# Chunk 2 of a fused kernel: transposes on the matmul engine against a transposed load normalised in place

## The chip, the cores and the metric

The kernel runs on one core of one Trainium2 chip. The metric is the device time of one execution in microseconds, as a median of three runs. Five engines run their own queues of instructions in program order: TensorE (matmuls, PE in the profile; PEld is its loading of weights), VectorE (DVE), ScalarE (ACT), GpSimd (POOL) and SyncE (SP, which here only starts transfers). They wait for each other by semaphores.

## The reference, cut to what matters

```python
xn = layernorm(q)                                  # (1, 2048, 448), over the last axis
# branch A
k_shift = sum(k_pad[:, t:t + S] * shift_k[:, 3 - t] for t in range(4))
kv = k_shift * v
y  = irfft(rfft(kv, 2S) * rfft(ssm_k, 2S))[:S] + kv * ssm_D      # long causal convolution
A  = xn * y
# branch B
h   = xn @ w1 + b1                                 # 448 -> 1792
B   = (h * tanh(softplus(h))) @ w2                 # 1792 -> 448
return q + A + B
```

Everything is float32. There are S = 2048 positions and D = 448 columns.

## The kernel before, in words

**The dense branch.** The 2048 positions are cut into 8 chunks of 256 (`CH`), each chunk into two halves `jj` of 128. For each chunk the 1792 hidden columns are handled in 7 pairs of 128-column blocks. So there are 56 pairs; pair `i` is chunk `i // 7`, block pair `i % 7`. A float32 product is done as three products of rounded parts: weights are held as `w1h`, `w1l`, `w2h`, `w2l`, the normalised input as `XH` and `XL`, the activations as `ach` and `acl`. "High" is a rounded copy made by ScalarE, "low" is the rest, made by VectorE with a subtraction.

The program is a list of half steps, the slots `s`, written out by hand. Pair `i` has slots `2i` and `2i + 1`. In the even one TensorE does the first product, `g1_mm(i)` (L513). In the odd one ScalarE does the activation, `mish(i)` (L521) and the rounded copy (L85), VectorE the low part `acl` (L86), and TensorE the second product of the pair two steps back, `g2_mm(i - 2)` (L545 to L547), which sums over a chunk's 7 pairs in two accumulators `pg2`, one for each half. There are two such buffers in all, so a chunk's first `g2_mm` has to wait until the sum of the chunk before has been read. That is done by `g2_evac` (L552, VectorE): it adds the accumulators into the tile `Q[c]`, which holds the chunk of q. For chunk `c` it stands at the start of slot 14c + 18, one half step behind the last `g2_mm` of the chunk. `g2_out` then writes `Q[c]` out, and its buffer (there are three) goes to chunk `c + 3`.

**Two ways to the transposed input.** TensorE needs the normalised chunk with its columns on the partitions. Chunks below `NT` (3) go by the *transposes*: q is loaded (`ln_load`), VectorE takes mean and variance (L407, L410, L413), GpSimd raises to the power -0.5 (L416) and normalises (L420, L424), then `ln_T` transposes each half by four matmuls against an identity (L465) into an accumulator bank, from which ScalarE copies `XH` (L477) and VectorE subtracts `XL` (L475). Chunks from `NT` on go by a *transposed load*: `xT_load` reads q already transposed on the host (512 KB, L435), `nt_stats` takes the same moments, `nt_store` writes mean and factor to a scratch in memory (2 KB, `MR`, L443), `nt_row` reads them back as a row broadcast to all partitions (L446, 128 KB, one for each half) into `idr`, `nt_norm` subtracts and multiplies by the row (two VectorE operations of 128x512 a half, L452), and `nt_split` makes `XH` (L459) and `XL` (L460). The rows lie in the same tile as the identity, behind the constants `f1`.

The slots of these steps come from `NT_AT`, `NT_SOON` or an entry of `NT_HOW`: counted from `b`, the start of the chunk before (one slot behind it for chunks below 5), `q` is the slot of `ln_load`, `x` of `xT_load`, `stats` of the moments, `flush` of the slot by which they are all in the queue, and `row`, `norm` and `split` have one slot for each half. Moments are put into a list, `drip`; a call `dv()` behind most VectorE operations takes one of them out.

**The convolution branch** shares the first half of the time. `h` (the filter) and `kv` are brought to the frequency domain in 8 groups each: `f1_mm` (L147, TensorE, into the banks `pq` and `pr`), `f1_fold` (L153 ScalarE, then two VectorE operations, L157), `f1_out` (a transfer to `Dh` or `Dkv`). A kv group first needs the four taps and the product with v: VectorE operations L190 to L203, the last of them L203; one multiplication of each group is handed to GpSimd (`taps_pool`, L183). The groups' slots are `H_AT` and `KV_AT`; kv group 7 has slot 59. From slot 66 on come the frequency products (`hv_mm`, `prod`, `i1_mm`), and at the end the way back (`i2_mm`, `gate`).

Within a slot the queues get: `plan` of that slot, the products and activations, then `plan2` of that slot ("after"). Engines run far apart: VectorE is often a few us behind, SP as far ahead as buffers allow.

Of the kernel before, what the change touches and what calls it, by code (L numbers as in the profile page):

```python
# [17 lines left out]
NP = NF // 2  # L18
# [11 lines left out]
I2_AT = {100: ((6, 7, 0, 1), 92, (95, 97, 98, 99), (0, 2, 0, 1)),  # L30
         108: ((2, 3, 4, 5), 101, (104, 105, 106, 107), (0, 1, 0, 1))}
LATE = 2
NT = 3
NT_AT = {"q": -5, "x": -1, "stats": -2, "flush": 0, "row": (4, 8), "norm": (7, 10), "split": (8, 11)}
NT_SOON = dict(NT_AT, row=(4, 5), norm=(4, 7), split=(6, 8))
NT_HOW = {c: NT_SOON for c in (4, 7)}
NT_HOW[3] = dict(NT_SOON, q=-9, stats=-3, flush=-2)
NT_HOW[5] = dict(NT_AT, q=-8, stats=-4, flush=-2)
WARM_N = (448, 448, 448)
FILL_N = (224, 112, 96)  # L40

# [2 lines left out]
def tile_kernel(ctx: ExitStack, tc, q, qT, k, v, sk, hT, sD, w10, w1, w2, c_fib, c_g, c_gi, c_i2, out):  # L44
# [20 lines left out]
    E = dp.tile([NJ * 4, 64, D], F32, name="E")  # L65
    MR = {c: dp.tile([2, CH], F32, name="MR") for c in range(NT, NCHUNK)}

# [8 lines left out]
    def rs(c):  # L76
        return rstd[:, 2 * c:2 * c + 2] if c < NT else mv[:, 2 * c:2 * c + 2, 1]

# [26 lines left out]
    def dv(n=1):  # L105
        for _ in range(n):
            if drip:
                drip.pop(0)()
# [193 lines left out]
    def late(c):  # L302
        return c >= NCHUNK - LATE
# [84 lines left out]
    def ln_load(c, eng=None):  # L388
        Q[c] = mp.tile([128, 2, D], F32, name="qt", tag="qt", bufs=3)
        if c:  # L390
            nc.sync.dma_start(Q[c], q[:, 2 * c:2 * c + 2])
        else:
            for jj in range(2):
                nc.sync.dma_start(Q[c][:, jj], q[:, jj])

    def xn_tile():
        return mp.tile([128, 4, CH], F32, name="xn", bufs=1)

    def ln_parts(c):
        st = mp.tile([128, 2, 6], F32, name="bst", bufs=2)  # L400
        ve = mp.tile([128, 2], F32, name="ve", bufs=2)
        if c < NT:
            XN[c] = xn = xn_tile().rearrange("p a b -> p (a b)").rearrange("p (j d) -> p j d", j=2)
# [24 lines left out]
    def ln_stats(c):  # L428
        stats, aggr, eps, power, norm, tail, ve = ln_parts(c)
        drip.extend([lambda: stats(0), lambda: stats(1), lambda: aggr(0), lambda: aggr(1), lambda: eps(0, 2),  # L430
                     lambda: [f(*a) for f, *a in ((power, 0, 2), (norm, 0), (tail, 0, 1), (norm, 1), (tail, 1, 2))]])
# [47 lines left out]
    def ln_T(c, jj):  # L479
        if jj == 0:  # L480
            dv(len(drip))
            x_tiles(c)
        p = pg()
        transposes(c, jj, p)
        for lo in range(2):
            x_split(c, jj, p, lo)
# [4 lines left out]
    pairs = [(c, p) for c in range(NCHUNK) for p in range(NP)]  # L491

    def g1_mm(i):
        c, p = pairs[i]
        XH, XL = XS[c]
        pt = [(bank(GB[i]) if i in GB else pg()).rearrange("p (a b) -> p a b", a=2) for _ in range(2 if i == 0 else 1)]
        ps = [pt[n % len(pt)][:, n] for n in range(2)]
        mm = [[], []]
        for n in range(2):
            f = 2 * p + n  # L500
            fs = slice(128 * f, 128 * f + 128)
            hh, hl, lh = ([(w[:, kt, fs], x[:, kt]) for kt in range(3)] for w, x in ((w1h, XH), (w1h, XL), (w1l, XH)))
            th, tl = ((w1h[:, 3, fs], x[:, 3]) for x in (XH, XL))
            mm[n] = [(n, *m) for m in hh + lh + [th] + hl + [tl]]

            if 0 < i < NP:
                mm[n] = [(n, *m) for m in hh + hl + lh + [th, tl]]
        if i == 0:
            seq = mm[0][:7] + mm[1][:3] + mm[0][7:] + mm[1][7:10] + mm[1][3:7] + mm[1][10:]
        else:  # L510
            seq = mm[0] + mm[1]
        for n_, (n, l, r) in enumerate(seq):
            nc.tensor.matmul(ps[n], l, r, start=all(m[0] != n for m in seq[:n_]), stop=all(m[0] != n for m in seq[n_ + 1:]))  # L513
        P1[i] = ps

    def mish(i):
        p = pairs[i][1]
        ps = P1.pop(i)
        a = mp.tile([128, 2, CH], F32, name="a", bufs=2)
        for n in range(2):  # L520
            nc.scalar.activation(a[:, n], ps[n], AF.Mish, bias=b1t[:, 2 * p + n:2 * p + n + 1])  # L521
            if i == n == 0:
                w1_hi(2)
        if i == 0:
            w1_lo(2)
        ah = mp.tile([128, 2, CH], F32R, name="ach", bufs=3)
        al = mp.tile([128, 2, CH], F32R, name="acl", bufs=3)
        AHL[i] = ah, al
        if 2 * i + 1 in hv:
            held.append(lambda: split(ah, al, a))  # L530
        else:
            split(ah, al, a)
            dv()

    def g2_mm(i, jjs=(0, 1)):
        c, p = pairs[i]
        ah, al = AHL[i]
        for n in range(2):
            f = 2 * p + n
            for jj in jjs:  # L540
                if f == 0:
                    P2[c, jj] = g2p.tile([128, 512], F32, name="pg2")
                ps = P2[c, jj][:, :D]
                cs = slice(128 * jj, 128 * jj + 128)
                nc.tensor.matmul(ps, ah[:, n, cs], w2h[:, f], start=f == 0, stop=False)  # L545
                nc.tensor.matmul(ps, ah[:, n, cs], w2l[:, f], start=False, stop=False)  # L546
                nc.tensor.matmul(ps, al[:, n, cs], w2h[:, f], start=False, stop=f == NF - 1)  # L547

    def g2_evac(c, jjs=(0, 1)):
        x = Q[c]  # L550
        for jj in jjs:
            V.tensor_add(x[:, jj], P2.pop((c, jj))[:, :D], x[:, jj])  # L552
            dv()
            if late(c):
                nc.sync.dma_start(out[:, 2 * c + jj], x[:, jj])
# [4 lines left out]
    def mlp_slot(s):  # L560
        i, half = divmod(s, 2)
        n = len(pairs)
        j = i - G2_LAG
        if half == 0:
            if i < n:
                c, p = pairs[i]
                if c + 1 < NT:
                    if p == 0:
                        ln_load(c + 1)
                    if p == (3 if c in (0, 2) else 2):  # L570
                        ln_stats(c + 1)
                    if c == 0:
                        dv(len(drip))
                    if p == NP - 1:
                        ln_T(c + 1, 1)
                g1_mm(i)
        else:
            if i < n:
                c, p = pairs[i]
                if p == NP - 2 and c + 1 < NT:  # L580
                    ln_T(c + 1, 0)
                if s not in hv:
                    mish(i)
            if 0 <= j < n - 1:
                g2_mm(j)
            elif j == n - 1:
                for jj in range(2):
                    g2_mm(j, (jj,))
                    g2_evac(pairs[j][0], (jj,))
# [43 lines left out]
    for o in range(NO):  # L633
        s, d = OCT_AT[0] + OCT_AT[1] * o, OCT_AT[1]
# [33 lines left out]

    for c in range(NT, NCHUNK):
        at_ = NT_HOW.get(c, NT_AT)  # L670
        b = 2 * NP * (c - 1) + (1 if c < 5 else 0)
# [19 lines left out]
    warm = g2p.tile([128, 512], F32, name="pg2")  # L691
    for n in WARM_N:
        nc.tensor.matmul(warm[0:8, 0:n], wz, wz[:, 0:1].to_broadcast([128, n]), start=True, stop=True)
# [49 lines left out]
    plan.setdefault(5, []).insert(0, (f1_out, (Dh, H_HEAD, "h", nc.gpsimd)))  # L743
    for s in range(nslots):
        j = s // 2 - G2_LAG - 1
        if s % 2 == 0 and j >= 0 and pairs[j][1] == NP - 1:
            g2_evac(pairs[j][0])
        if s in hv:
            mish(s // 2)
        for fn, args in plan.pop(s, ()):  # L750
            fn(*args)
        mlp_slot(s)
        fns = plan2.pop(s, ())
        for fn, args in fns:
            if fn is i1_out:
                fn(*args)
        for fn, args in fns:
            if fn is not i1_out:
                fn(*args)
# [69 lines left out]
```

## Time and profile before

| | |
|---|---|
| median of 3 runs | 359.3 us (358.9 to 359.31) |
| the profiled execution | 359.25 us, of which the span from first to last instruction is 357.4 |
| mean granted TensorE clock | 0.998 |
| TensorE busy | 351.4 us, 98% |
| VectorE busy | 270.6 us, 76% |
| ScalarE busy | 156.8 us, 44% |
| GpSimd busy | 73.1 us, 20% |
| moved by DMA | 83.27 MB, 233 GB/s |

The span is also cut in 40 equal slices of 8.9 us, with a digit for the busy tenths of each. A group of instructions has its line, engine, operation, the tiles written and read, the shape, a count, and behind the bar the busy us and the mean ns of one; behind the second bar stands the engine's idle time just before them, and what ended it. In a timeline a row has its start, its length and the same names; two instructions of one kind in succession share a row (x2). Matmuls overlap, so the cost of one is read from the distance between starts, not from its length.

### The profile page before, as it was taken

What the parts mean: (1) busy time and instruction counts of PE and PEld (TensorE: products, weight loads), DVE (VectorE), ACT (ScalarE), POOL (GpSimd) and SP (SyncE); (2) the same over time, 40 slices, a digit from 0 to 9 for tenths busy, and PEclk for the clock granted to TensorE, in tenths of its full rate; (3) what the DMA queues carried; (4) which work ended last, traced back from release to release, by engine and by line L of the source; (5) the groups of instructions that cost most, each with busy time, mean ns of one, the idle gap of its engine ahead of it and who ended that gap; (6) DMA issues with size and microseconds to landing.
All of it is one profiled execution on the core that took longest, in us unless ns stands there. A gap on an engine that the chain in (4) does not pass through costs nothing.

```text
span 357.4 us, 7437 instructions
## 1 busy us (share of the span) xinstructions
PE 351.4 (98%) x3092; PEld 289.6 (81%) x3092; DVE 270.6 (76%) x375; ACT 156.8 (44%) x267; POOL 73.1 (20%) x78
## 2 busy tenths in 40 slices
PE   8999999999999999999999999999999999999995
PEld 2988888888888988888987757766775699979794
DVE  5989748999999999999537756756963933788941
ACT  3976652344243242342333453445445443354470
POOL 2037002942220240212000031011031116040030
PEclk9999999999999999999999999999999999999999
DMA  7998976949659537664869669999895387989086
GB/s 245 340 388 294 408 297 167 348 120 265 201 166 314 164 108 168 222 160 105 243 203 342 220 169 296 242 275 311 282 265 122 84 237 275 405 312 281 19 117 140
DMA packets 30691, 83.27 MB, mean 233 GB/s; under 512 B 3137, under 2 KB 15810, under 8 KB 30658
## 3 DMA queue, kind: packets, MB, share of 16 engines
q1 hardware_dynamic: 21842, 47.82, 39.7%
q0 software_dynamic: 4928, 22.95, 22.7%
q10 hardware_dynamic: 3888, 12.03, 12.8%
q8 instruction: 24, 0.39, 0.4%
q14 instruction: 9, 0.07, 0.1%
HBM read 54.34 MB, written 28.45 MB: 232 GB/s over the span
## 4 chain that ended last, share of the span: by engine, by line
PE 94%; DMA 2%; DVE 1%; ACT 1%; SPq 0%; issue 0%
PE pg L513 22%; PE pg L545 13%; PE pg L547 12%; PE pg L546 12%; PE pq L513 7%; PE pp L513 5%; PE pr L513 4%; PE pq L147 4%; PE pr L236 3%; PE pp L236 3%; PE pp L275 2%; DMA kr<-in_w_dram 2%; PE pq L236 2%; PE pr L275 1%; PE pp L329 1%; DVE st L157 1%
## 5 line engine op out<-in xcount | busy, mean ns | idle before, releaser
L545 PE MATMUL pg<-w2h,ach 128*128 128x448 f32 x224 | 82.6, 369 | 0.6 <-DVE qt L552 0.6
L547 PE MATMUL pg<-w2h,acl 128*128 128x448 f32 x224 | 81.4, 363 | 0.0
L546 PE MATMUL pg<-w2l,ach 128*128 128x448 f32 x224 | 81.2, 362 | 0.0
L86 DVE TENSOR_TENSOR acl<-a,ach 128x512 fp32r<-128x512 f32 x56 | 38.5, 688 | 32.1 <-ACT ach L85 31.8
L521 ACT ACTIVATE a<-pg,b1t 128x256 f32<-128x256 f32 x66 | 27.9, 473 | 66.6 <-PE pg L513 46.7
L513 PE MATMUL pg<-XH,w1h 128*128 128x256 f32 x264 | 52.8, 283 | 0.1
L545 PEld LDWEIGHTS pg<-w2h,ach 128*128 128x128 f32 x224 | 41.9, 187 | 12.2 <-issue 7.9
L513 PEld LDWEIGHTS pg<-XH,w1h 128*128 128x128 f32 x264 | 41.4, 188 | 7.2 <-issue 5.6
L547 PEld LDWEIGHTS pg<-w2h,acl 128*128 128x128 f32 x224 | 42.1, 188 | 2.4
L546 PEld LDWEIGHTS pg<-w2l,ach 128*128 128x128 f32 x224 | 42.1, 188 | 2.4
L513 PE MATMUL pg<-XL,w1h 128*128 128x256 f32 x264 | 42.9, 277 | 0.0
L157 DVE TENSOR_TENSOR st<-pq,st 128x896 f32<-128x896 f32 x32 | 34.8, 1087 | 4.5 <-ACT st L153 3.9
L513 PEld LDWEIGHTS pg<-XL,w1h 128*128 128x128 f32 x264 | 35.9, 188 | 0.0
L85 ACT CAST ach<-a 128x512 fp32r<-128x512 f32 x56 | 34.8, 621 | 1.7
L513 PE MATMUL pg<-XH,w1l 128*128 128x256 f32 x198 | 33.5, 278 | 0.0
L183 POOL TENSOR_TENSOR x<-kr,skb 128x896 f32<-128x896 f32 x8 | 17.0, 2129 | 68.2 <-PE pr L147 26.2
L513 PEld LDWEIGHTS pg<-XH,w1l 128*128 128x128 f32 x198 | 27.6, 188 | 0.0
L200 DVE TENSOR_TENSOR x<-x 128x896 f32<-128x896 f32 x24 | 26.2, 1090 | 1.6 <-POOL x L183 0.8
L521 ACT ACTIVATE a<-pq,b1t 128x256 f32<-128x256 f32 x20 | 8.4, 472 | 31.8 <-PE pq L513 31.8
L286 POOL DMA_DIRECT2D E<-qe x14 | 8.7, 629 | 63.1 <-ACT qe L283 63.1
L153 ACT COPY st<-pr 128x896 f32<-128x896 f32 x16 | 14.5, 907 | 14.1 <-PE pr L147 8.2
L416 POOL TENSOR_TENSOR mv<-ve,mhalf 128x2 f32<-128x2 f32 x5 | 5.0, 1008 | 72.0 <-DVE ve L413 72.0
(138 smaller groups left out, 608.5 us busy)
## 6 DMA issues: line engine op xcount, KB each, us to landing
Dkv<-st ACTq DMA_DIRECT2D x16, 448.0 KB, 5.3
ah<-Dh SPq DMA_DIRECT2D x8, 896.0 KB, 7.7
av<-Dkv SPq DMA_DIRECT2D x8, 896.0 KB, 8.5
e<-E POOLq DMA_DIRECT2D x8, 896.0 KB, 7.3
E<-qe POOLq DMA_DIRECT2D x14, 448.0 KB, 6.3
kr<-in_k_dram SPq DMA_DIRECT2D x10, 448.0 KB, 6.2
Dh<-st ACTq DMA_DIRECT2D x10, 448.0 KB, 6.6
x<-in_hT_dram SPq DMA_DIRECT2D x8, 448.0 KB, 6.1
```

The costliest lines, as they stand in the source:

```text
L85: nc.scalar.copy(h, raw)
L86: V.tensor_sub(l, raw, h)
L153: nc.scalar.copy(st[:, 1], o)
L157: f(st[:, n], e, st[:, 1])
L183: nc.gpsimd.tensor_mul(o, KR[g - u // 2], skb[:, u:u + 1].to_broadcast([128, 2, D]))
L200: V.tensor_add(KV[g], KV[g], o)
L236: nc.tensor.matmul(p[32 * t:32 * t + 32, r, :D], g[rs, t, c], a[rs, t], start=True, stop=True, tile_position=(64 * r, 32 * t))
L513: nc.tensor.matmul(ps[n], l, r, start=all(m[0] != n for m in seq[:n_]), stop=all(m[0] != n for m in seq[n_ + 1:]))
L521: nc.scalar.activation(a[:, n], ps[n], AF.Mish, bias=b1t[:, 2 * p + n:2 * p + n + 1])
L545: nc.tensor.matmul(ps, ah[:, n, cs], w2h[:, f], start=f == 0, stop=False)
L546: nc.tensor.matmul(ps, ah[:, n, cs], w2l[:, f], start=False, stop=False)
L547: nc.tensor.matmul(ps, al[:, n, cs], w2h[:, f], start=False, stop=f == NF - 1)
```

## The change

Chunk 2 goes by the transposed load instead of the transposes (`NT` is 2). Its steps are those of `NT_SOON`, with the splits in other slots. As `b` is 15 for chunk 2, this gives: `ln_load` slot 10 (before, 14), the moments in slots 13 to 15 (before, from 18), `xT_load` slot 14, the rows in slots 19 and 20, the normalisation behind slots 19 and 22, the splits behind slots 23 and 25. Before, the transposes stood in slots 25 and 26. Chunk 2's first product is in slot 28, as before.

And `g2_evac` of chunk 2 (`EVAC_SOON`) is moved from the start of slot 46 to the end of the products of slot 45, behind the last `g2_mm` of the chunk; so it stands ahead of what follows slot 45.

```diff
-NT = 3
+NT = 2
 NT_AT = {"q": -5, "x": -1, "stats": -2, "flush": 0, "row": (4, 8), "norm": (7, 10), "split": (8, 11)}
 NT_SOON = dict(NT_AT, row=(4, 5), norm=(4, 7), split=(6, 8))
 NT_HOW = {c: NT_SOON for c in (4, 7)}
+NT_HOW[2] = dict(NT_SOON, split=(8, 10))
 NT_HOW[3] = dict(NT_SOON, q=-9, stats=-3, flush=-2)
 NT_HOW[5] = dict(NT_AT, q=-8, stats=-4, flush=-2)
+EVAC_SOON = 2,
...
             if 0 <= j < n - 1:
                 g2_mm(j)
+                if pairs[j][1] == NP - 1 and pairs[j][0] in EVAC_SOON:
+                    g2_evac(pairs[j][0])
...
-        if s % 2 == 0 and j >= 0 and pairs[j][1] == NP - 1:
+        if s % 2 == 0 and j >= 0 and pairs[j][1] == NP - 1 and pairs[j][0] not in EVAC_SOON:
             g2_evac(pairs[j][0])
```

## The prediction

> **What bounds the kernel now.** I read the page first, then busy time by stretch, then the waits and the timeline where engines meet.
>
> ```profile
> span 357.4 us, 7437 instructions
> ...
> PE 351.4 (98%) x3092; PEld 289.6 (81%) x3092; DVE 270.6 (76%) x375; ACT 156.8 (44%) x267; POOL 73.1 (20%) x78
> ...
> DVE  5989748999999999999537756756963933788941
> ...
> PE 94%; DMA 2%; DVE 1%; ACT 1%; SPq 0%; issue 0%
> ```
>
> By the page TensorE is the bound: 98% busy, 94% of the chain. But VectorE's digits are nines from the 8th slice to the 19th (8.9 us each), so its 76% is a mean of two regimes. The same by stretch (columns: PE, PEld, DVE, ACT, POOL busy us, clock, DMA share, GB/s):
>
> ```profile
> 40.00:53.60 13.60, 13.60 (x103) 12.22 (x103) 7.01 (x8) 6.91 (x12) 0.00 (x0) 1.00 0.84 339
> 53.60:61.40 7.80, 7.80 (x64) 6.61 (x63) 6.64 (x14) 2.40 (x5) 0.93 (x1) 1.00 0.69 176
> 61.40:168.60 107.20, 106.65 (x813) 95.10 (x811) 104.72 (x148) 38.84 (x72) 32.02 (x19) 1.00 0.65 193
> 168.60:353.00 184.40, 184.40 (x1832) 146.00 (x1832) 117.82 (x152) 81.47 (x136) 27.50 (x40) 1.00 0.80 234
> ```
>
> From 61.40 to 168.60 both engines are full: TensorE idles 0.55 us, VectorE 2.48 us in 107.20. Before it VectorE is half idle (7.01 of 13.60), behind it TensorE never stops. Which of the two sets the pace in the full stretch is seen where TensorE waits for VectorE:
>
> ```profile
> PEld pq L147 <- DVE x L203: 0.2, 1, 0.2
> ```
> ```profile
> 167.51 1.09 DVE L203 TENSOR_TENSOR x<-x 128x896 f32<-128x896 f32 x1
> ```
> ```profile
> 168.66 0.59 PE L147 MATMUL pq<-x,con 32*64 32x448 f32 x2
> ```
> ```profile
> 135.84 1.14 DVE L552 TENSOR_TENSOR qt<-pg,qt 128x448 f32<-128x448 f32 x2
> ```
> ```profile
> 136.60 0.44 PE L545 MATMUL pg<-w2h,ach 128*128 128x448 f32 x1 [0.55 <-DVE qt L552]
> ```
>
> The last kv product (group 7, L203) ends at 168.60; its first-stage matmuls start at 168.66 and are listed as having waited for it. So at 168.6 TensorE has no slack against VectorE. At 136.60 it even stands 0.55 us, waiting for chunk 2's sum with q to free the accumulator of chunk 3. VectorE's queue runs without a real break from the fold at 61.40 to the product at 168.60, and it is VectorE's sum of work there that decides.
>
> **The change, part by part.** *TensorE loses chunk 2's eight transposes.*
>
> ```profile
> 73.88 0.60 PE L465 MATMUL pg<-con,xn 128*128 128x128 f32 x4
> 74.23 0.45 PE L545 MATMUL pg<-w2h,ach 128*128 128x448 f32 x1
> 74.52 0.37 PE L546 MATMUL pg<-w2l,ach 128*128 128x448 f32 x1
> 74.72 0.36 PE L547 MATMUL pg<-w2h,acl 128*128 128x448 f32 x1
> ...
> 77.76 0.66 PE L465 MATMUL pg<-con,xn 128*128 128x128 f32 x4
> 78.17 0.60 PE L513 MATMUL pg<-XH,w1h 128*128 128x256 f32 x3
> ```
>
> Start to start the two groups hold 0.35 (73.88 to 74.23) and 0.41 us (77.76 to 78.17); the first product behind the first takes 0.29 instead of the 0.20 of its neighbour. About 0.85 us, all on TensorE.
>
> *VectorE gets four normalising operations (L452), and its statistics move forward.*
>
> ```profile
> 47.60 0.69 DVE L86 TENSOR_TENSOR acl<-a,ach 128x512 fp32r<-128x512 f32 x1 [2.59 <-ACT ach L85]
> ...
> 61.40 1.09 DVE L157 TENSOR_TENSOR st<-pq,st 128x896 f32<-128x896 f32 x1 [1.09 <-ACT st L153]
> ...
> 64.63 0.69 DVE L86 TENSOR_TENSOR acl<-a,ach 128x512 fp32r<-128x512 f32 x1
> 65.24 0.98 DVE L193 TENSOR_TENSOR x<-kr,skb 128x448 f32<-128x448 f32 x1
> ...
> 70.52 0.97 DVE L193 TENSOR_TENSOR x<-kr,skb 128x448 f32<-128x448 f32 x1
> ...
> 77.68 0.62 DVE L193 TENSOR_TENSOR x<-kr,skb 128x448 f32<-128x448 f32 x1
> ...
> 103.88 1.41 DVE L452 TENSOR_TENSOR xn<-xn,con 128x512 f32<-128x512 f32 x2
> 105.22 1.08 DVE L157 TENSOR_TENSOR st<-pq,st 128x896 f32<-128x896 f32 x1
> ```
> ```profile
> 63.98 0.62 ACT L85 CAST ach<-a 128x512 fp32r<-128x512 f32 x1
> ```
> ```profile
> 63.53 3.37 POOL L420 TENSOR_SCALAR xn<-qt,mv,rstd 128x448 f32<-128x448 f32 x1
> ...
> 67.96 4.21 POOL L420 TENSOR_SCALAR xn<-qt,mv,rstd 128x448 f32<-128x448 f32 x1
> ```
> ```profile
> L460 DVE TENSOR_TENSOR XL<-xn,XH 128x512 fp32r<-128x512 f32 x10 | 6.9, 687 | 3.2 <-ACT XH L459 3.1
> ...
> L407 DVE BATCH_NORM_STATS2 bst<-qt 128x6 f32<-128x448 f32 x16 | 9.6, 618 | 2.8 <-DMA qt<-in_q_dram 2.7
> ```
> ```profile
> 81.00 0.68 DVE L475 TENSOR_TENSOR XL<-pg,XH 128x512 fp32r<-128x512 f32 x1
> ```
> ```profile
> 83.26 0.52 PE L513 MATMUL pg<-XH,w1h 128*128 128x256 f32 x3
> ```
>
> A pair of L452 holds VectorE 1.34 us (103.88 to 105.22). The statistics, now in slots 18 to 20, go to slots 13 to 15, into the 2.59 us idle before 47.60: free. The first pair stands after slot 19, just ahead of the fold at 61.40, where VectorE idles 1.09 us for ScalarE's copy; the two leaving statistics add 0.62 each, so 1.34 fits: free, with 1.09 + 1.24 − 1.34 = 1.0 us left. The second pair stands after slot 22, behind the product at 68.92 (a row below) and so inside the full stretch: +1.34. The two XL subtractions stay at the same price (0.69 against 0.68 us); they only read SBUF instead of an accumulator, as does ScalarE's cast ahead of each, and ScalarE has time (38.84 of 107.20).
>
> A wait could arise where chunk 2's first products need its low halves. The last XL now starts at 81.00; in the new order it stands behind the same products and comes 0.6 us later, done by 82.3. TensorE starts the chunk at 83.26 now, 0.85 sooner then, so at 82.4, and takes seven products of the high halves first, some 0.8 us at the spacing of this row's three (0.52 for three with the last one's run-out). Covered, by 0.8 us or so.
>
> What comes back: twice in this stretch L193 takes 0.98 and 0.97 us where its like takes 0.62, each time while GpSimd normalises chunk 2 (63.53 to 66.90, 67.96 to 72.17). Those two operations go away, and with them 0.36 + 0.35 = 0.71 us. A short operation ahead of 64.63 leaves too, but there VectorE waits for ScalarE's cast (63.98 + 0.62 = 64.60), so that gives nothing. Net for VectorE at 168.6: 1.34 − 0.71 = **+0.63 us**. Bounds: −0.1, if GpSimd cost other rows as much again; +1.34, if the two long rows have another cause.
>
> [...]
>
> *The sum with q of chunk 2* (L552 at 135.84) goes ahead of one 896-column product in VectorE's queue (of the size of L190's, 1.08 us, in a row below), and the write of its result and the reload of its buffer move with it. With VectorE late by 0.63 it still starts some 0.4 us sooner than now, which shortens the wait at 136.60. But TensorE then only arrives earlier at 168.66, where it waits for L203: worth nothing at the end. The same holds for the 0.85 us of transposes.
>
> *Queues.*
>
> ```profile
> L416 POOL TENSOR_TENSOR mv<-ve,mhalf 128x2 f32<-128x2 f32 x5 | 5.0, 1008 | 72.0 <-DVE ve L413 72.0
> ```
> ```profile
> DMA to landing us min/median/max: 3.8/5.2/10.0
> ```
> ```profile
> DMA to landing us min/median/max: 3.4/3.8/9.3
> ```
> ```profile
> 61.55 0.42 SPq L173 DMA_DIRECT2D kr<-in_k_dram  x1
> ```
> ```profile
> 68.92 1.08 DVE L190 TENSOR_TENSOR x<-kr,skb 128x896 f32<-128x896 f32 x1
> ```
> ```profile
> kr<-in_k_dram SPq DMA_DIRECT2D x10, 448.0 KB, 6.2
> ```
>
> GpSimd loses two normalisations and two copies of 64 columns and keeps the power. New transfers: the 512 KB of transposed q, the 2 KB of moments (L443, landing times 3.4/3.8/9.3) and two rows (L446, 3.8/5.2/10.0). GpSimd is empty from 40 to 53.6, so the moments leave by about 48.5 (47.6 at the latest for VectorE, 1.0 for the power), land at 52.3 and the row at 57.5, by medians. It is wanted at 59.1 (61.40 less the pair's 1.34 and the 1.0 left over); lateness up to 60.1 is free. The transposed q is asked for in slot 14, once chunk 1's last transposes have released its buffer, five slots ahead of use; the loads of h, k and v queued behind it on SP wait for that too, and are used three to nine slots later. Chunk 2's own q is asked for four slots sooner and passes the loads of slots 11 and 12 on SP, which land one place later, in a stretch in which VectorE is half idle. The second row waits on SP's queue for the first pair (60.4 by the above), ahead of the loads of q, h, k and v that follow there; I take 0.4 us later for them, one more issue of the length of the one shown. k at 61.55 lands at 67.8 by its median, then 68.2; VectorE wants it at 68.92 − 0.36 = 68.6. Hidden, by 0.4.
>
> **Sum.** The profiled execution took 359.25 us (span 357.4), the median is 359.3. The terms: transposes −0.85 and the wait at 136.6 up to −0.55, both used up by waiting at the last kv product; that product +1.34 − 0.71. TensorE starts group 7's matmuls 0.6 us later than at 168.66 and from there has no idle time to give (184.40 of 184.40): 359.25 + 0.6 = **359.8**.
>
> **Rivals.** (1) *Faster: TensorE keeps what it is relieved of.* That needs VectorE's last kv product to come at least 1.4 us sooner than I have it. Price: 0.85 + 0.55, so 357.8. For it: 98% and 94% of the page. Against: the wait at 168.66. [...] (2) *GpSimd's normalisation cost VectorE nothing:* the full 1.34, so 360.6. For it: most rows beside L420 have their usual length. (3) *Slower by a late row:* in a stretch with the DMA engines 0.84 busy the moments take their worst 9.3 us: 48.5 + 9.3 + 5.2 = 63.0 for the first row. It decides once the row lands behind 60.1; at 63.0 the fold that now starts at 61.40 starts at 64.3, 2.9 us late, of which nothing is made up before 168.6: 359.8 + 2.9 = 362.7.
>
> **How the numbers follow.** Forecast 0.55 (own range 359.3 to 360.4), rival 1 0.16, rival 2 0.18, rival 3 0.11. A measurement tells about 0.2% (0.7 us) from no change: 358.6 and 360.0 are the limits. The forecast lies close to the upper one and gives 0.38 within, 0.16 slower, 0.01 faster; rivals 2 and 3 are slower but for 0.01, rival 1 faster. So faster 0.17, same 0.39, slower 0.44. The range 358.4 to 361.2 takes in forecast, rival 2, half-kept gains and a slightly late row.
>
> **What would show it.** Right: no transposes between 73 and 79; L193 at 0.62 in both places; the last L203 ends near 169.2, with TensorE's wait before it of 1 us or so; the wait at 136.6 shorter or gone; VectorE idle under 2.5 us in its full stretch. Wrong: L203 ends before 168.6 (rival 1), or both L193 stay long (2), or the first L452 waits for con<-MR past 60.1 (3). A k load after 68.6 would add its lateness to all.

## The result, and the profile after

The changed kernel is slower: a median of 362.9 us (362.54 to 363.82, 4 runs) against 359.1 (358.9 to 359.31, 4 runs), a ratio of 1.0106 with the interval 1.0094 to 1.0119. The forecast was 359.8, the range 358.4 to 361.2. The profiled execution took 363.07 us, with a span of 361.1. The loss is not the clock's alone: three of the four executions after have a mean granted clock of 0.994 to 0.995, the fourth has 1.000 and took 362.54. In the kernel after, line numbers are two higher than in the kernel before.

VectorE's timeline after, from just behind chunk 2's moments to the last kv product (start, length, line, operation, and in brackets the idle time and what ended it):

```profile
47.31 0.69 DVE L88 TENSOR_TENSOR acl<-a,ach 128x512 fp32r<-128x512 f32 x1 [1.39 <-ACT ach L87]
...
60.12 1.42 DVE L454 TENSOR_TENSOR xn<-xn,con 128x512 f32<-128x512 f32 x2 [1.14 <-DMA con<-MR]
61.47 1.08 DVE L159 TENSOR_TENSOR st<-pq,st 128x896 f32<-128x896 f32 x1
...
65.48 0.62 DVE L195 TENSOR_TENSOR x<-kr,skb 128x448 f32<-128x448 f32 x1
...
71.21 1.09 DVE L192 TENSOR_TENSOR x<-kr,skb 128x896 f32<-128x896 f32 x1 [2.31 <-DMA kr<-in_k_dram]
72.22 1.41 DVE L454 TENSOR_TENSOR xn<-xn,con 128x512 f32<-128x512 f32 x2
...
74.15 0.62 DVE L195 TENSOR_TENSOR x<-kr,skb 128x448 f32<-128x448 f32 x1
...
171.28 1.09 DVE L205 TENSOR_TENSOR x<-x 128x896 f32<-128x896 f32 x1
```

Set against the same operations before, each start gives the lag so far, and each difference a term:

| operation | before | after | lag | what was added since the row above |
|---|---|---|---|---|
| low part `acl` | 47.60 | 47.31 | −0.29 | a different start of this execution |
| fold | 61.40 | 61.47 | +0.07 | 0.36: the first pair waits for its row |
| first long L193 | 65.24 | 65.48 | +0.24 | 0.17: mostly a gap of 0.20 behind GpSimd's multiplication |
| product L190 | 68.92 | 71.21 | +2.29 | 2.41 for k, −0.36 because L193 (now L195) takes 0.62, not 0.98 |
| second long L193 | 70.52 | 74.15 | +3.63 | 1.34: the second pair |
| last kv product | 167.51 | 171.28 | +3.77 | −0.35 for L193, +0.49 (below) |

The two executions differ by 363.07 − 359.25 = 3.82. So the loss is complete at the last kv product, and the largest part is one wait of VectorE for k. Why k was late is seen in the timelines of GpSimd, which sends the moments, and of SP, which starts the loads in its order:

```profile
47.04 0.77 POOL L445 DMA_DIRECT2D MR<-mv  x1 [0.29 <-POOL mv L418]
```
```profile
55.49 0.33 SPq L448 DMA_DIRECT2D con<-MR  x1
...
61.57 0.32 SPq L448 DMA_DIRECT2D con<-MR  x1
61.98 1.51 SPq L393 DMA_DIRECT2D qt<-in_q_dram  x1
63.59 0.37 SPq L135 DMA_DIRECT2D x<-in_hT_dram  x1
64.02 0.42 SPq L175 DMA_DIRECT2D kr<-in_k_dram  x1
```
```profile
DMA to landing us min/median/max: 3.6/6.0/8.4
```

The last line is the landing time of the six transfers of moments (L445). Chunk 2's left at 47.04 and allowed the first row at 55.49: 8.4 us, in a stretch in which the DMA engines are 0.89 busy (the windows below). The row so came to the first pair at 60.12. The second row goes into the same tile and waits in SP's queue until that pair has read it, to 61.57. Everything that SP has behind it waits too: k leaves at 64.02 instead of 61.55. These 2.47 us are 0.88 of waiting (61.57 less the 60.69 at which q was issued before), 0.41 for the row's own issue and 1.18 because the issue of q took 1.51 instead of 0.33. To this comes 1.0 from the transfer itself: k was used 7.19 after it left, where before it landed in 6.2. So it came 3.46 later than before (71.21 for 67.75), and VectorE, which was free for it at 68.9, waited 2.31.

The 0.49 is a wait that passes from engine to engine. The timelines of TensorE, VectorE and ScalarE, and the windows (columns as in the prediction):

```profile
79.22 0.59 PE L149 MATMUL pq<-x,con 32*64 32x448 f32 x2 [3.08 <-DVE st L159]
...
80.27 1.01 PE L515 MATMUL pg<-XH,w1h 128*128 128x256 f32 x3
...
84.36 0.36 PE L547 MATMUL pg<-w2h,ach 128*128 128x448 f32 x1
...
172.42 0.59 PE L149 MATMUL pq<-x,con 32*64 32x448 f32 x2 [0.75 <-DVE x L205]
```
```profile
92.45 0.69 DVE L88 TENSOR_TENSOR acl<-a,ach 128x512 fp32r<-128x512 f32 x1 [0.27 <-ACT ach L87]
...
93.76 2.22 DVE L159 TENSOR_TENSOR st<-pq,st 128x896 f32<-128x896 f32 x2 [0.62 <-ACT st L155]
```
```profile
84.56 0.84 ACT L523 ACTIVATE a<-pg,b1t 128x256 f32<-128x256 f32 x2 [3.26 <-PE pg L515]
...
87.46 3.42 ACTq L170 DMA_DIRECT2D Dh<-st  x2
```
```profile
40.00:53.60 13.60, 13.60 (x102) 12.21 (x101) 8.43 (x13) 6.94 (x12) 1.50 (x2) 1.00 0.89 348
...
61.40:168.60 107.20, 104.12 (x780) 92.59 (x779) 101.78 (x146) 38.88 (x72) 22.47 (x14) 0.98 0.63 189
...
80.01:83.42 3.41, 3.41 (x22) 3.15 (x15) 3.34 (x6) 0.91 (x1) 0.00 (x0) 0.50 0.46 139
...
172.40:356.00 183.60, 183.58 (x1827) 145.30 (x1828) 117.18 (x150) 80.83 (x135) 27.53 (x40) 1.00 0.79 233
```

TensorE waits 3.08 us at 79.22, in the first stage of `h` group 6, for VectorE's fold of kv group 0 to free the bank. Then the granted clock is 0.50 for 3.41 us, and the first product of one pair (22 matmuls, 80.27 to 84.36) takes 4.09 us, where the same one before took 2.68 (78.17 to 80.85). So TensorE is 3.51 us behind its time of before. This reaches VectorE through ScalarE's queue. ScalarE's activation at 84.56 waited for that product (before, 81.05), and the transfer `Dkv` behind it left at 85.50 instead of 81.98, close ahead of those of `Dh`. Issuing `Dh` then took ScalarE's queue 3.42 us instead of 2.62, and its next copy into `st` waited 0.41 until `Dkv` had landed. VectorE waits 0.27 and 0.62 us for ScalarE there, some 13 us behind TensorE's wait. From 172.42 on TensorE has no idle time, as before from 168.66; the 3.76 us stay to the end.

### The profile page after: what moved, and what is told of

Read it like the earlier page. It is cut to its first block, busy times and chain, and to the rows that moved or that the text cites. A ratio compares the mean times of both kernels' runs of the same rounds, so it can differ in the third digit from the quotient of the medians.

```text
span 361.1 us, 7423 instructions
## 1 busy us (share of the span) xinstructions
PE 352.4 (98%) x3084; PEld 290.4 (80%) x3084; DVE 273.0 (76%) x379; ACT 156.9 (43%) x267; POOL 64.2 (18%) x75
## 4 chain that ended last, share of the span: by engine, by line
PE 51%; issue 8%; DVE 6%; POOL 2%; DMA 1%; DVEq 0%
PE pq L515 7%; PE pg L547 7%; PE pg L549 7%; PE pg L548 6%; PE pp L515 5%; PE pr L515 4%; PE pr L238 3%; PE pp L238 3%; PE pp L277 2%; PE pg L515 2%; DVE x L202 2%; POOL x L185 2%; PE pq L238 2%; PE pr L277 1%; DMA xn<-in_qT_dram 1%
## 5 line engine op out<-in xcount | busy, mean ns | idle before, releaser
L515 PE MATMUL pg<-XH,w1h 128*128 128x256 f32 x264 | 53.6, 287 | 0.0
L515 PEld LDWEIGHTS pg<-XH,w1h 128*128 128x128 f32 x264 | 42.2, 192 | 7.8 <-issue 6.5
L418 POOL TENSOR_TENSOR mv<-ve,mhalf 128x2 f32<-128x2 f32 x6 | 5.8, 961 | 83.6 <-DVE ve L415 83.6
```

## The experiments

The theory: VectorE's queue sets the time up to 168.6, and the change makes it late above all through SP's queue, in which the second row holds up k. Rivals: the second pair's own work; the sooner sum with q; or no queue at all but transfers slowed by one more load. Times of "before" come from the runs beside each; all medians lie at 359.1 to 359.4.

**VectorE's work decides** (e5_product_twice): the kernel before, with one of its products run twice.

```diff
-            V.tensor_mul(o, KR[g - u // 2], skb[:, u:u + 1].to_broadcast([128, 2, D]))
+            for _ in range(2 if (g, u) == (1, 0) else 1):
+                V.tensor_mul(o, KR[g - u // 2], skb[:, u:u + 1].to_broadcast([128, 2, D]))
```

> The kernel before, with one VectorE operation of the full stretch (the first product of kv group 1, 128x896, start to start 1.0 us) done twice, its result the same. If VectorE's sum of work up to the last kv product decides the time: 1.0 us more, 360.1 (359.8 to 360.3). If TensorE decides and VectorE has slack: no change, 359.1.

Measured: 360.21 us (360.06 to 360.62, 7 runs), ratio 1.0029 (1.0019 to 1.004), 0.9 us for an operation of 1.1 (1.0 from start to start). VectorE's timeline:

```profile
64.42 1.05 DVE L86 TENSOR_TENSOR acl<-a,ach 128x512 fp32r<-128x512 f32 x1
65.39 0.61 DVE L194 TENSOR_TENSOR x<-kr,skb 128x448 f32<-128x448 f32 x1
...
67.70 1.49 DVE L204 TENSOR_TENSOR x<-x 128x896 f32<-128x896 f32 x1
69.11 2.20 DVE L191 TENSOR_TENSOR x<-kr,skb 128x896 f32<-128x896 f32 x2
...
168.50 1.09 DVE L204 TENSOR_TENSOR x<-x 128x896 f32<-128x896 f32 x1
```

The last product comes 0.99 us later than at 167.51, and TensorE can make up none of it. The rows also show what GpSimd's normalisation costs: it is still there, but the two long rows are now `acl` (1.05 for 0.69) and L204 (1.49 for 1.09). In both executions one VectorE operation is stretched during each of GpSimd's two: by 0.36 and 0.35 us before, by 0.36 and 0.40 here.

**The sum with q alone** (e3_evac_only): the kernel before with `EVAC_SOON`, chunk 2 still by the transposes.

```diff
-NT = 2
+NT = 3
-NT_HOW[2] = dict(NT_SOON, split=(8, 10))
```

> The kernel before with only the sum of chunk 2 with q half a step sooner. If VectorE's last kv product decides: TensorE waits less at 136.6 and more at 168.7, 359.1 us (within 0.3). If TensorE has slack there: 0.55 us less, 358.6.

Measured: 358.89 us (358.75 to 359.03, 11 runs), ratio 0.9988 (0.9979 to 0.9996). TensorE's wait before the product at 136.6 is gone, and its timeline shows where it went:

```profile
168.19 0.59 PE L148 MATMUL pq<-x,con 32*64 32x448 f32 x2 [0.62 <-DVE x L204]
```

TensorE gains half a us and waits it out at the last kv product. VectorE's last product is at 167.04, 0.47 sooner than before; 0.32 of that stands already at its operation of 47.28, ahead of the edit. So the edit gave 0.15 in this execution. The medians differ by 0.41; how much of that is the edit is not shown.

**The same sum, late** (e4_evac_late): the changed kernel without `EVAC_SOON`.

```diff
-EVAC_SOON = 2,
+EVAC_SOON = ()
```

> The changed kernel with chunk 2's sum with q back at the start of slot 46, so only the transposed load and VectorE's normalisation are changed. If VectorE's last kv product decides, the sum's place in VectorE's queue is worth nothing or 0.3 us: 362.9 us (362.4 to 363.4). If the sooner sum is itself part of the loss (it now stands ahead of a product that kv group 5 needs): 0.5 us or more under the changed kernel.

Measured: 364.16 us (363.02 to 365.21, 5 runs), ratio 1.0137 (1.0115 to 1.0159): the moved sum isn't where the loss comes from. The time is above the expected 362.4 to 363.4. Its waits for k (2.13 us) and of TensorE at the same place (3.20 us) are those of the changed kernel; TensorE also waits 0.61 at 142.16 for the sum. Its profiled execution of 365.05 us has a mean granted clock of 0.50 from 78.80 to 85.62, for 6.82 us, and VectorE's two waits for ScalarE behind it are 1.26 and 1.02 us, where the changed kernel has 0.27 and 0.62.

**The second row behind k** (e1_row_behind_k): the changed kernel with the second row two slots later, so that SP issues q, h and k first.

```diff
-NT_HOW[2] = dict(NT_SOON, split=(8, 10))
+NT_HOW[2] = dict(NT_SOON, row=(4, 7), split=(8, 10))
```

> The changed kernel, with the transfer of chunk 2's second row three places later in SP's queue, behind the loads of q, h and k that it stood in front of. Theory A (the queue): that row waits for the first pair of normalising operations, and the k load of kv group 1 waits behind it, so VectorE stands 2.31 us in its full stretch; with the order changed k lands by 69, the wait of 2.31 us is gone and with it the 0.9 us of idle that TensorE's stall behind it brought, so 360.0 us (359.5 to 360.8). Theory B (VectorE's added work and the added transfers): the loads are late because the DMA engines are busier, whatever the order; k still lands near 71 and the time stays within 0.7 us of the changed kernel's 362.9.

Measured: 360.9 us (359.64 to 363.17, 12 runs), ratio 1.0056 (1.0037 to 1.0076). SP's and VectorE's timelines:

```profile
61.47 0.33 SPq L393 DMA_DIRECT2D qt<-in_q_dram  x1
...
62.33 0.42 SPq L175 DMA_DIRECT2D kr<-in_k_dram  x1
62.86 0.98 SPq L448 DMA_DIRECT2D con<-MR  x1
```
```profile
60.43 1.42 DVE L454 TENSOR_TENSOR xn<-xn,con 128x512 f32<-128x512 f32 x2 [1.45 <-DMA con<-MR]
61.78 1.09 DVE L159 TENSOR_TENSOR st<-pq,st 128x896 f32<-128x896 f32 x1
...
69.12 1.08 DVE L192 TENSOR_TENSOR x<-kr,skb 128x896 f32<-128x896 f32 x1
...
168.52 1.09 DVE L205 TENSOR_TENSOR x<-x 128x896 f32<-128x896 f32 x1
```

With the order of the queue turned, k is no longer waited for, and 2 us of the 3.8 are back. This execution starts 0.27 sooner than before's (47.33 for 47.60), its fold is 0.65 late on that, and its last product comes 1.01 later: the rest, 1.01 + 0.27 − 0.65 = 0.63, is the forecast's net price of the pair. The median stays above the forecast because the first row is late here too, and because the executions spread: the five of 361.9 us and more have mean clocks of 0.994 to 0.998, the other seven 0.999 and 1.0.

**The queue held up in the kernel before** (e9_queue_block): nothing of the change, only a small transfer in SP's queue, ahead of h and k, that waits for VectorE.

```diff
+    Dx = dp.tile([128, 256], F32, name="Dx")
+    plan.setdefault(21, []).insert(0, (lambda: nc.sync.dma_start(Dx, ST["h", 5][:, 1, 0, 0:256]), ()))
```

> The kernel before, with one small transfer more on SP's queue (128x256 of the folded h group 5, to a scratch nobody reads), ahead of the loads of h group 6 and k group 1; it cannot start until VectorE has ended that fold at 63.6, so those loads go out some 2.5 us later, as in the changed kernel. No work is added on any engine. Theory A: k is issued at 64.4 and lands at 70.3 to 71, VectorE stands 1.4 to 2.1 us for it in its full stretch, 361.0 us (360.5 to 361.7). Theory B (VectorE's added work makes the time): 359.3.

Measured: 362.14 us (361.87 to 362.67, 4 runs), ratio 1.0084 (1.0071 to 1.0097). SP's and VectorE's timelines:

```profile
63.44 0.33 SPq L682 DMA_DIRECT2D Dx<-st  x1
...
64.59 0.54 SPq L173 DMA_DIRECT2D kr<-in_k_dram  x1
```
```profile
71.79 1.09 DVE L190 TENSOR_TENSOR x<-kr,skb 128x896 f32<-128x896 f32 x1 [2.58 <-DMA kr<-in_k_dram]
```

Here k leaves 3.04 us later than before, VectorE waits 2.58 for it, and 2.95 us arrive at the end, above the expected 360.5 to 361.7. No operation was added to any engine, only the transfer of 128 KB. So being held up in SP's queue is enough for a loss of this size. Here too k took 7.2 us and not 6.2.

**Without the second pair** (e2_no_pair2): its row is still fetched, chunk 2's second half goes on without subtraction and factor.

```diff
+        if (c, jj) == (2, 1):
+            return
```

> The changed kernel without the two normalising operations of chunk 2's second half (that half goes on unnormalised); rows and queues as they are. Theory A: the wait for k stays, only the pair's 1.34 us and some of the idle behind it go, 361.2 us (360.7 to 361.8). Theory B (it is VectorE's added work that costs): nothing of VectorE's work in the full stretch is left over that before had not, so back at the time of before or under it, 358.4 to 359.3 us.

Measured: 361.12 us (361.02 to 361.62, 5 runs), ratio 1.0057 (1.0044 to 1.007): 1.8 less than the changed kernel. VectorE's timeline still has

```profile
70.62 1.09 DVE L192 TENSOR_TENSOR x<-kr,skb 128x896 f32<-128x896 f32 x1 [1.83 <-DMA kr<-in_k_dram]
```

and SP's has

```profile
62.27 0.42 SPq L175 DMA_DIRECT2D kr<-in_k_dram  x1
```

The wait isn't the pair's doing, and the pair costs its own length on top: 1.34, and 0.48 by which the wait is shorter here, make the 1.8. But neither is this wait mainly the queue's. k left only 0.72 later than before and was used 8.35 us after; in e1 it left at 62.33 and was there, without a wait, when VectorE came to it 6.79 us after. So the third rival, slower transfers, holds in part: it is most of the lateness here and 1.0 of 3.46 in the changed kernel. What slowed k is not settled.

**A place of its own for the second row** (e6_row_buffer, and the same kernel once more as e6_again): SP need not wait for the first pair. The row goes to the first half of `XL`, which is still empty.

```diff
+    def row_of(c, jj):
+        return XS[c][1][:, 0].bitcast(F32) if (c, jj) == (2, 1) else idr
...
-        nc.sync.dma_start(idr, MR[c][jj].partition_broadcast(128))
+        if (c, jj) == (2, 1):
+            x_tiles(c)
+        nc.sync.dma_start(row_of(c, jj), MR[c][jj].partition_broadcast(128))
```

> The changed kernel, with chunk 2's second row in a place of its own (the low halves of chunk 2, not yet written then), so that its transfer waits for nothing on VectorE; its place in SP's queue as in the changed kernel. Theory A (the wait in SP's queue): the loads behind it go out at 61.5, k lands by 68.5, no wait of VectorE for k; the first row still comes about 0.7 us late; the second pair's 1.34 less GpSimd's 0.71 stays: 360.3 us (359.8 to 360.8). Theory B (the added transfers and VectorE's added work make the time, not the queue's order): within 0.7 us of 362.9.

> The kernel of e6_row_buffer, once more, for a profile: its executions lay between 360.0 and 364.2 us while the kernel before stayed within 0.7. If the spread is in the landing of the moments, of the first row or of k in the full DMA stretch, a longer execution shows VectorE waiting longer for con<-MR or kr; if it is in TensorE's clock alone, those waits stay as they were at 360.0.

Measured: 361.76 us (360.03 to 364.15, 6 runs), ratio 1.0089 (1.006 to 1.0117), and 363.24 for the single run. The median lies between the two theories, and the executions do not agree: the two profiled ones are 3.2 us apart. That of 360.03 has no wait for k, 1.45 us of TensorE idle time in all from 61.40 to 168.60, and a clock of 1.0. That of 363.24 shows on VectorE and TensorE:

```profile
61.00 1.42 DVE L459 TENSOR_TENSOR xn<-xn,con 128x512 f32<-128x512 f32 x2 [1.78 <-DMA con<-MR]
...
70.82 1.09 DVE L192 TENSOR_TENSOR x<-kr,skb 128x896 f32<-128x896 f32 x1 [1.07 <-DMA kr<-in_k_dram]
```
```profile
78.84 0.59 PE L149 MATMUL pq<-x,con 32*64 32x448 f32 x2 [2.44 <-DVE st L159]
```

The first pair started 1.1 later than in the other, k was issued at 63.79 against 61.84, and the clock was 0.50 from 80.26 to 83.68. SP's issue of the load of h took 1.16, where the other had 0.37. The same program has both: what differs is when transfers land and how long SP takes to issue them, and behind the longer waits the clock. Why one execution has this and another not is not shown.

**Everything sooner** (e7_early_pairs): that buffer, the moments two slots earlier, both rows at once, the pairs behind slots 17 and 19.

```diff
-NT_HOW[2] = dict(NT_SOON, split=(8, 10))
+NT_HOW[2] = dict(NT_SOON, stats=-4, flush=-4, row=(2, 2), norm=(2, 4), split=(8, 10))
```

> The same as e6_row_buffer, with chunk 2's moments two slots sooner (all in slot 11), both rows asked for in slot 17, and the pairs behind slots 17 and 19, so that all four normalising operations lie ahead of the fold at 61.4, where VectorE still idles. Theory A: nothing is added in VectorE's full stretch, GpSimd's 0.71 us goes out of it, k lands in time: VectorE's last kv product comes 0.2 to 0.7 us sooner than before the change, 358.8 us (358.3 to 359.3). Theory B: the transposed load costs by its transfers, wherever VectorE does the work: over 360.

Measured: 360.64 us (359.5 to 360.85, 5 runs), ratio 1.0034 (1.0022 to 1.0046). The rows were issued at 47.26 and 47.68, no wait for k is left, and both pairs stand ahead of the full stretch. But VectorE reached its fold only at 63.12:

```profile
49.63 0.69 DVE L88 TENSOR_TENSOR acl<-a,ach 128x512 fp32r<-128x512 f32 x1 [4.92 <-ACT ach L87]
...
61.64 1.41 DVE L459 TENSOR_TENSOR xn<-xn,XL 128x512 f32<-128x512 f32 x2
...
63.12 2.22 DVE L159 TENSOR_TENSOR st<-pq,st 128x896 f32<-128x896 f32 x2
```

It had waited 4.92 for ScalarE at 49.63, whose queue was issuing `Dh` until 48.06 (before, until 45.76) and started its activation at 48.11, and had no idle time left for the second pair. The expected gain wasn't there. The time is the "over 360" of theory B, but the trace has no wait for the rows.

**The transposed load behind the rows** (e10_load_behind_rows): with that buffer, the 512 KB out of the way of the moments.

```diff
+NT_HOW[2] = dict(NT_SOON, row=(2, 2), x=3, norm=(4, 4), split=(8, 10))
```

> The changed kernel with the second row in a place of its own (as in e6_row_buffer), both rows asked for in slot 17 and the 512 KB of transposed q behind them on SP's queue, and both pairs behind slot 19. If what made the first row late is the added 512 KB ahead of the moments, in the stretch from 38 to 55 us in which landings take 8 us and more: the moments land by 52.5, the rows by 57, both pairs run between 59.0 and 61.7, the fold starts 0.5 us late and GpSimd's 0.71 comes back, so 359.1 us (358.7 to 359.7). If the moments are late for another reason: they land near 55 as in the changed kernel, the pairs start at 60 or later, and the time is over 360.

Measured: 362.85 us (362.06 to 363.07, 5 runs), ratio 1.0096 (1.0083 to 1.011). The moments left at 46.95 and the first row at 53.31, 6.36 us later, where the changed kernel has 8.45 between the two. With the 512 KB behind them they are sooner, as expected; but the wait moved to the large load, and the expected gain wasn't there:

```profile
62.39 1.42 DVE L459 TENSOR_TENSOR xn<-xn,con 128x512 f32<-128x512 f32 x2 [3.42 <-DMA xn<-in_qT_dram]
```

**Only GpSimd's work less** (e8_half_on_act): the kernel before, with ScalarE copying chunk 2's second half in GpSimd's place, without normalising it.

```diff
+            if (c, jj) == (2, 1):
+                nc.scalar.copy(xn[:, jj, :D], Q[c][:, jj])
+                return
```

> The kernel before, with the second half of chunk 2 not normalised: ScalarE copies it instead of GpSimd's operation of 4.21 us at 67.96. If GpSimd's operation stretched VectorE's L193 at 70.5 from 0.62 to 0.97 us: that row takes 0.62 and the time is 0.35 us less, 358.9. If that row had another cause: it stays 0.97, 359.3.

Measured: 358.58 us (358.44 to 358.98, 11 runs), ratio 0.9984 (0.9976 to 0.9993). VectorE's two rows:

```profile
64.85 0.98 DVE L193 TENSOR_TENSOR x<-kr,skb 128x448 f32<-128x448 f32 x1
...
70.18 0.61 DVE L193 TENSOR_TENSOR x<-kr,skb 128x448 f32<-128x448 f32 x1
```

The row whose GpSimd operation is gone has its usual length, the other not. That is the forecast's reading of the long rows. Of the 0.6 us, 0.36 are this row; most of the rest stands before it (the fold at 61.01, 0.39 ahead of before's).

**ScalarE normalises chunk 2** (e11_act_norm, e12_act_norm_behind): the transposes stay and so do VectorE's other operations; GpSimd keeps the power and two tiny operations, ScalarE does each half in one activation. With `EVAC_SOON`.

```diff
+                nc.gpsimd.tensor_tensor(nm, mv[:, 4:6, 0], rs(c), op=ALU.mult)
+                nc.gpsimd.tensor_tensor(nm, wz[:, 0:2], nm, op=ALU.subtract)
...
+                    nc.scalar.activation(XN[c][:, jj, :D], Q[c][:, jj], AF.Identity, bias=nm[:, jj:jj + 1], scale=rs(c)[:, jj:jj + 1])
```

In e11 these stand where GpSimd's stood, in e12 behind slot 21's activation.

> The kernel before (transposes kept), with chunk 2's sum with q half a step sooner and chunk 2 normalised by ScalarE (one activation with scale and bias for each half, two small operations of GpSimd for the bias) instead of GpSimd. If VectorE's last kv product decides and GpSimd's two normalisations cost it 0.71 us: both L193 take 0.62, that product comes 0.7 us sooner, TensorE's eight transposes stay, 358.3 us (357.9 to 358.7). If not: 358.9, as with the sooner sum alone.

> As e11_act_norm, with ScalarE's two normalising activations behind the activation and the rounded copy of slot 21 instead of ahead of them (there ScalarE stood 3.36 us for GpSimd's factor with the step's activation behind it, and VectorE 2.91 us for the copy). If VectorE's last kv product decides: no wait of that kind, both L193 at 0.62 us, that product 0.7 us sooner than with the sooner sum alone: 358.3 us (357.9 to 358.6). If GpSimd's normalisation cost VectorE nothing: 358.9.

Measured: e11 361.01 us (360.83 to 361.53, 5 runs), ratio 1.0046 (1.0033 to 1.0058); e12 **358.47** (358.12 to 358.76, 11 runs), ratio 0.998 (0.9971 to 0.9989). ScalarE's timeline of e11, and VectorE's of e12:

```profile
64.75 1.42 ACT L427 ACTIVATE xn<-qt,ve,rstd 128x448 f32<-128x448 f32 x2 [3.36 <-POOL ve L426]
```
```profile
65.35 0.62 DVE L196 TENSOR_TENSOR x<-kr,skb 128x448 f32<-128x448 f32 x1
...
70.32 0.62 DVE L196 TENSOR_TENSOR x<-kr,skb 128x448 f32<-128x448 f32 x1
...
166.97 1.09 DVE L206 TENSOR_TENSOR x<-x 128x896 f32<-128x896 f32 x1
```

In e11 ScalarE stands 3.36 us for GpSimd's factor, and the activation and the copy behind it, which VectorE needs, stand too. Some instructions further on the same work hides. In e12 both long rows are short, and the last product comes 0.54 sooner than before, in an execution that starts 0.11 later (47.71 for 47.60): 0.65 us, near the 0.71 of the two rows, though the sooner sum has a part in it (0.15 in e3). e12 is faster than both kernels. Against e3, 358.89 in another set of runs on another chip, the two gains differ by 0.27 us (0.68 and 0.41 below their own before); that difference was not measured side by side.

## Why the prediction was wrong

**What bounds the kernel: right.** VectorE's queue decides up to the last kv product (e5, e8, e12), and TensorE's savings end as a wait there (0.62 us in e3, 0.75 after). Rival 1 is out, though the page gives TensorE 98% after the change as before it. What did change on the page is TensorE's share of the chain, 94% before and 51% after:

```profile
PE 51%; issue 8%; DVE 6%; POOL 2%; DMA 1%; DVEq 0%
```

The share tells which way the chain runs and not the time: e12, which is faster than both, has 52%.

**The costs on VectorE: right.** The second pair took 1.34 us and the two L193 gave back 0.71; e1 has the net at 0.63. Rival 2 is out. In e5, too, beside GpSimd's operations of 2.77 us each, the two long operations are stretched by 0.36 and 0.40.

**"Queues": the step that failed.** Three sizes in it were wrong. The moments were given their median of 3.8 us, and took 8.4. The first pair was so expected at 59.1 and started at 60.12. The second row's place ahead of q, h and k was priced at one issue, 0.4 us, against a margin of 0.4; it cost 2.47: that issue (0.41), the wait for the late first pair (0.88), and q's long issue (1.18). And k was given its median of 6.2 us, and took 7.2. The forecast named k as what would show it wrong, with 68.6 as the limit and 68.2 as its own value; k came at 71.2, and VectorE's 2.31 us of idle time in its full stretch are the main term of the miss. With the order turned (e1) the term is gone; with the queue held up alone (e9) the loss is there; e2 shows that a slow landing of k makes it too. Not settled is why SP's issue of q took 1.51 us where the same took 0.33 before. Such long issues turn up in other runs at other loads (1.16 for h in e6_again, 1.49 for v in e9).

The issuing itself was no small part: of the 2.47 us that k lost in SP's queue, 1.59 (0.41 and 1.18) went into it, over a fifth of the 7.2 from k's issue to its use. The other 0.88 are waiting behind a transfer that could not start. No run here started these loads from another engine.

**Rival 3 had the size, not the path.** It gave 362.7 for a first row landing at 63.0. The row came at 60.1, at the edge of what the forecast called free, and made the fold 0.36 late. What it did to k through the queue was nowhere in it.

**TensorE's wait at 79.22: not foreseen.** The fold of kv group 0 comes behind k's lateness, the second pair, and now also the first XL subtraction (76.35). The forecast counted the time that VectorE loses, but looked for TensorE's waits only at chunk 2's first products (83.26), 136.6 and 168.66. This one gave 0.49 net; in e4, where the clock stayed low longer, the waits that came back to VectorE were longer too.

## What to carry to other kernels

When a step puts a transfer that waits into an in-order queue, price it by how late the thing that it waits for can be, and then ask who is behind it; a margin of 0.4 us for a load is no margin where the same load was there within 6.79 us of its issue in one run (e1) and was used 8.35 after it, with a wait of 1.83, in another (e2). Work moved out of the bounding engine's way pays only if its inputs are there when the new queue comes to it: the kernel with two activations more in ScalarE's queue was 1.6 us slower than before with them in one place, and 0.7 faster with them a few instructions later (both with the sooner sum, which alone was 0.4 faster). And follow a delay of the bounding engine to the other engines' waits: behind TensorE's wait of 3.08 us in the changed kernel the granted clock was 0.50 for 3.41 us more.

## What the hardware did that was not expected

After a wait of 3.08 us, TensorE's granted clock stood at 0.50 for 3.41 us (80.01 to 83.42); with a wait of 3.20 in e4 for 6.82 (from 78.80, while it still waited), after 2.44 in e6_again for 3.42. After another wait of 2.44 (e10, at 72.5) it stayed at 1.00. In the changed kernel the first product of the pair that ran in that stretch took 1.41 us longer (4.09 for 2.68). What decides whether the clock falls is not shown: a wait of 2.44 us stands once with such a period behind it and once without.
